# One 8 MB load per V in a decode attention kernel: longer runs, a single V buffer, and a new order of products

## The chip, the cores and the metric

The kernel runs on one core of a Trainium2 chip. The metric is device time in microseconds (us), the median of several runs. Lower is better. PE is TensorE, DVE is VectorE, ACT is ScalarE, SP is SyncE, which issues all the large loads here.

## The reference, cut to what matters

One token of a decode step is computed: attention of 32 query heads over a cache of 8 K/V heads with 32768 positions each, a small gated FFN, and a mix of both.

```python
Hq, Hkv, Sk, Dh = 32, 8, 32768, 128          # bf16; k_cache and v_cache: 64 MB each
q = (x @ wq).reshape(B, Sq, Hq, Dh)...       # wq 512 x 4096
scores = einsum("bhqd,bhkd->bhqk", q, k) * Dh ** -0.5
o = einsum("bhqk,bhkd->bhqd", softmax(scores), v)
a = o.reshape(B, Sq, Hq * Dh) @ wo           # wo 4096 x 512
b = (silu(x @ w_gate) * (x @ w_up)) @ w_down # 512 x 1792, 1792 x 512
return g * a + (1 - g) * b                   # g = sigmoid(sum(x * gate_w))
```

148 MB have to be read once, with little arithmetic on each byte.

## The kernel before

Everything large is loaded by SP in one fixed order, `stream`, into a ring of five slots of 4 MB (32 KB in each of 128 partitions). An entry whose slot was used by an earlier entry first waits until that one is released.

```python
stream = [("wq",), ("K", 0, 0), ("F1",), ("K", 0, 1), ("F2",)]
for g in range(1, G):
    for hf in range(2):
        stream += [("K", g, hf), ("V", g - 1, hf)]        # halves of K and V alternate
stream += [("V", G - 1, 0), ("V", G - 1, 1), ("wo",)]
place = {("wq",): 1, ("F1",): 4, ("wo",): 2}
for g in range(G):
    for hf in range(2):
        place["K", g, hf] = 2 * hf                        # slots 0 and 2
        place["V", g, hf] = 2 * hf + 1                    # slots 1 and 3
place["V", G - 1, 1] = 0
...
for i, e in enumerate(stream):                            # on SP, in order
    if e in before:
        sp.wait_ge(*released[before[e]])
```

`F1` is w_gate and w_up, `F2` is w_down (in memory of its own). PE takes a K half (transposes on PE, copies by DVE, scores on PE), then the products of a V half of the head before:

```python
with pe.Fori(0, G) as g:
    emit_k(0)
    with pe.If(g > 0):
        emit_pv(0)              # 32 products, V half 0 of head g - 1
    with pe.Else():
        emit_ffn()              # gate and up products
        pe.wait_ge(sem_t1, 2)
    emit_k(1)
    with pe.If(g > 0):
        emit_pv(1)
    emit_max()                  # maximum of head g: PE -> DVE -> PE -> DVE, short steps
```

After the loop come the products of the last V, the normalisation, and the products with wo, which lands in five pieces.

## Time and profile before

| | before |
|---|---|
| time, median (range) | 352.43 us (352.38 to 352.46) |
| the large DMA queue, share of 16 engines' span | 98.5% |
| PE, DVE busy | 74%, 57% |
| packets of the queue, first to last | 1.75 to 347.75 us |

The page of the profile cuts the span into 40 slices. These are, of the kernel before, the slices of PE's clock (tenths), of the DMA engines' busy share (tenths) and of the rate, and the line of the large queue (packets, MB, share of the 16 engines' span):

```profile
PEclk9999999899989698989789698989769987999899
DMA  8999999999999999999999999999999999999995
GB/s 337 441 402 434 422 440 426 443 441 422 422 437 441 430 422 426 445 441 422 422 434 445 430 422 426 441 441 422 426 422 452 434 422 426 437 445 422 413 419 207
q1 hardware_dynamic: 6050, 148.12, 98.5%
```

DMA is at 9 from the second slice to the last but one: the kernel is bound by its load queue. The chain that ended last, of the same page (shares of the span by engine, then by line), says so from the other side:

```profile
DMA 7%; PE 3%; SPq 0%; DVE 0%; issue 0%
DMA ring<-in_A_wo_dram 7%; PE ps L404 2%; PE ps L418 1%; SPq L288 0%; DVE ktT L732 0%; DVE row L824 0%; PE ps L569 0%; PE ps L465 0%
```

It is the last piece of wo, which waited its turn in the queue. Anything else on that chain is small.

The order of PE near the end, from the timeline (start us, duration us, engine, line, operation, out<-in, count):

```profile
320.38 0.63 PE L418 MATMUL ps<-ktT,qc 128*32 128x512 bf16 x8 [0.95 <-DVE ktT L732]
320.84 1.90 PE L485 MATMUL ps<-ring,ET 128*16 128x512 bf16 x32
322.67 0.27 PE L450 MATMUL ps<-ident_f,pmax 128*1 128x128 f32 x1
323.51 0.35 PE L454 MATMUL ps<-gm,ones_f 1*128 1x4 f32 x2 [0.57 <-PEq L317]
328.60 3.38 PE L485 MATMUL ps<-ring,ET 128*16 128x512 bf16 x32 [0.92 <-PEq L317]
```

The last scores of the last K half (320.38) are followed at once by the second half's 32 products of the head before (320.84). The last line is the first half of the last V: its 32 products took 3.38 us and not 1.90, after PE had hardly worked. The issues of SP in the timeline of the same kernel:

```profile
281.96 0.33 SPq L306 DMA_DIRECT2D ring<-in_A_k_cache_dram  x1
283.93 22.16 SPq L306 DMA_DIRECT2D ring<-in_A_v_cache_dram  x2
306.14 0.43 SPq L299 DMA_DIRECT2D ring<-in_A_v_cache_dram  x1
320.81 2.24 SPq L288 DMA_DIRECT2D ring<-in_A_wo_dram  x5
```

The line of 283.93 holds two issues: the second half of V(6), the V of the last head but one, at 283.93, and the first half of the last V, V(7), at 305.8 us. The second half of V(7) follows in two parts from 306.14 (one of them shown) and wo at 320.8, while the packets of V(6) are still under way until 318. The queue never runs dry.

### The profile page before, as it was taken

The page shows a single profiled execution, that of the slowest core. Times are in us where ns is not written, and L with a number is a line of the kernel's source. Part 1 is how long each engine was busy: PE and PEld are TensorE (multiplying, and loading weights), DVE is VectorE, ACT ScalarE, POOL GpSimd, SP SyncE. Part 2 cuts the span into 40 slices and gives each one's busy share as a digit, 9 for nine tenths or more (in the row PEclk, how much of TensorE's full clock was granted, in tenths as well). Part 3 has the DMA queues.
Part 4 walks back from the last instruction along what each step waited for, and adds up shares of the span by engine and source line. Part 5 has one row for each costly group of instructions (what it writes and reads, how often), then busy time and mean ns, then how long its engine had stood idle before and what let it go on. Part 6 is the DMA issues. An engine that isn't in the chain of part 4 may idle for free. (4 is left out here: it accounts for less than half of the span.)

```text
span 350.6 us, 5679 instructions
## 1 busy us (share of the span) xinstructions
PE 259.2 (74%) x2423; PEld 179.1 (51%) x2423; DVE 200.1 (57%) x368; ACT 19.9 (6%) x57; POOL 1.4 (0%) x8
## 2 busy tenths in 40 slices
PE   0449876989495886858595978858597939777686
PEld 0147153856282846546382847546474718454342
DVE  4148287779284675838283765748265926666210
ACT  1100000300100002000100001000100010000100
POOL 1000000000000000000000000000000000000000
PEclk9999999899989698989789698989769987999899
DMA  8999999999999999999999999999999999999995
GB/s 337 441 402 434 422 440 426 443 441 422 422 437 441 430 422 426 445 441 422 422 434 445 430 422 426 441 441 422 426 422 452 434 422 426 437 445 422 413 419 207
DMA packets 6060, 148.20 MB, mean 423 GB/s; under 512 B 675, under 2 KB 678, under 8 KB 1062
## 3 DMA queue, kind: packets, MB, share of 16 engines
q1 hardware_dynamic: 6050, 148.12, 98.5%
q8 instruction: 4, 0.07, 0.1%
q14 instruction: 2, 0.02, 0.0%
q10 hardware_dynamic: 4, 0.00, 0.0%
HBM read 148.11 MB, written 0.00 MB: 422 GB/s over the span
## 5 line engine op out<-in xcount | busy, mean ns | idle before, releaser
L732 DVE COPY ktT<-ps 128x1024 bf16<-128x1024 bf16 x256 | 163.1, 684 | 81.8 <-PE ps L404 79.2
L404 PE MATMUL ps<-ident_f,ring 128*128 128x128 f32 x1024 | 157.9, 310 | 48.0 <-PEq L317 48.0
L404 PEld LDWEIGHTS ps<-ident_f,ring 128*128 128x128 f32 x1024 | 132.9, 161 | 80.5 <-issue 57.1
L418 PE MATMUL ps<-ktT,qc 128*32 128x512 bf16 x512 | 41.6, 401 | 15.2 <-DVE ktT L732 15.1
L485 PE MATMUL ps<-ring,ET 128*16 128x512 bf16 x512 | 32.0, 393 | 2.8 <-PEq L317 2.1
L485 PEld LDWEIGHTS ps<-ring,ET 128*16 128x16 bf16 x512 | 12.5, 91 | 19.1 <-issue 7.6
L418 PEld LDWEIGHTS ps<-ktT,qc 128*32 128x32 bf16 x512 | 7.9, 95 | 28.0 <-DVE ktT L732 24.2
L737 DVE TENSOR_REDUCE pmaxf<-ps 128x1 f32<-128x512 f32 x16 | 11.1, 691 | 13.8 <-DVEq L736 13.8
L589 ACT ACTIVATE qc<-qz 128x112 bf16<-128x112 bf16 x8 | 2.4, 296 | 197.7 <-DVE gsel L755 194.2
L502 PEld LDWEIGHTS ps<-osel,pv_sb 128*128 128x128 f32 x80 | 11.9, 228 | 1.4 <-DVE pv_sb L773 1.0
L621 ACT ACTIVATE P<-ps,nbias 128x512 bf16<-128x512 f32 x16 | 10.8, 676 | 29.0 <-DVE gsel L755 29.0
L502 PE MATMUL ps<-osel,pv_sb 128*128 128x4 f32 x80 | 11.3, 265 | 0.8 <-DVE pv_sb L773 0.5
L773 DVE COPY pv_sb<-ps 128x512 f32<-128x512 f32 x10 | 6.8, 682 | 6.5 <-PE ps L485 6.5
L465 PE MATMUL ps<-ident,P 128*128 128x128 bf16 x72 | 7.0, 219 | 1.7 <-ACT P L621 1.2
L767 DVE COPY ET<-ps 128x512 bf16<-128x512 bf16 x18 | 7.5, 414 | 1.3 <-PE ps L465 1.3
L372 PE MATMUL ps<-ring,xT 128*1 128x448 bf16 x32 | 6.6, 984 | 0.0
L747 DVE TENSOR_REDUCE gm<-ps 1x4 f32<-1x128 f32 x8 | 2.2, 279 | 7.7 <-DVEq L746 7.7
L465 PEld LDWEIGHTS ps<-ident,P 128*128 128x128 bf16 x72 | 5.4, 98 | 2.1 <-ACT P L621 1.3
L345 PE MATMUL ps<-ring,xT 128*1 128x512 bf16 x32 | 3.6, 626 | 3.6 <-PEq L317 3.6
L454 PE MATMUL ps<-gm,ones_f 1*128 1x4 f32 x16 | 2.8, 243 | 4.6 <-PEq L317 4.6
L326 PE MATMUL ps<-ones_bf,x_row 1*128 1x1 bf16 x4 | 0.3, 173 | 7.9 <-DMA gw_row<-in_gate_w_dram 7.9
L692 DVE CAST ring<-ps 128x512 bf16<-128x512 f32 x2 | 1.3, 685 | 7.5 <-PE ps L345 7.5
(70 smaller groups left out, 50.3 us busy)
## 6 DMA issues: line engine op xcount, KB each, us to landing
ring<-in_A_k_cache_dram SPq DMA_DIRECT2D x16, 4096.0 KB, 25.1
ring<-in_A_v_cache_dram SPq DMA_DIRECT2D x15, 4096.0 KB, 32.8
ring<-in_A_wq_dram SPq DMA_DIRECT2D x1, 4096.0 KB, 12.3
ring<-in_A_v_cache_dram SPq DMA_DIRECT2D x2, 2048.0 KB, 29.4
ring<-in_A_wo_dram SPq DMA_DIRECT2D x1, 2048.0 KB, 22.4
ring<-in_B_w_gate_dram SPq DMA_DIRECT2D x1, 1792.0 KB, 25.3
ring<-in_B_w_up_dram SPq DMA_DIRECT2D x1, 1792.0 KB, 29.2
wd_t<-in_B_w_down_dram SPq DMA_DIRECT2D x1, 1792.0 KB, 43.3
```

The lines of the kernel that those rows point to most:

```text
L345: ins = pe.matmul(ps_q[i][32 * c : 32 * c + 1, :], xT[:, k : k + 1], wq_v[:, k, n0 : n0 + 512], start=(k == 0), stop=(k == KC - 1),)
L372: ins = pe.matmul(acc[32 * c : 32 * c + 1, :], xT[:, k : k + 1], wt[:, k, c * FW : (c + 1) * FW].rearrange("d (i j) -> d j i", j=FC), star ...
L404: ins = pe.transpose(stb[:, t * 64 : (t + 2) * 64], two.bitcast(FP32), ident_f[:, :])
L418: ins = pe.matmul(ps_sc[hf][32 * c : 32 * c + 32, :], qc[:, e, 24 - PB * i : 56 - PB * i], kt[:, e, :], start=(i == 0 and e == 0), stop=(i ...
L465: ins = pe.transpose(ps_pt[:, hf * 512 + m * 128 : hf * 512 + (m + 1) * 128], P[:, hf, m * 128 : (m + 1) * 128], ident[:, :],)
L485: ins = pe.matmul(ps_pv[32 * c : 32 * c + 2 * PB, :], ET[:, hf, col : col + 2 * PB], src[:, i0 : i0 + 2, c, 2 * m : 2 * m + 2, :].rearrang ...
L502: ins = pe.matmul(ps_m[:, M_OT : M_OT + HPG], pv_sb[:, r * DH : (r + 1) * DH], osel[:, r * HPG : (r + 1) * HPG], start=(r == 0), stop=(r = ...
L621: act.activation(P[:, hf, :], ps_sc[hf], ACT.Exp, bias=nbias[:, 0:1], scale=SCALE, accum_out=esum[:, g, hf : hf + 1],).then_inc(sem_exp, 1)
L732: dve.tensor_copy(ktT[:, q % NKT, :], pst[q % NST]).then_inc(sem_cp, 1)
L737: ins = dve.tensor_reduce(pmaxf[:, hf : hf + 1], ps_sc[hf], AX.X, ALU.max)
L767: dve.tensor_copy(ET[:, hf, :], ps_pt[:, hf * 512 : (hf + 1) * 512]).then_inc(sem_ptc, 1)
L773: dve.tensor_copy(pv_sb[:, :], ps_pv).then_inc(sem_pvc, 1)
```

## The change

The intent is to read V in longer runs. A V of a head becomes one load of 8 MB with 64 KB contiguous in each partition, into two neighbouring slots. For the rows of K and V to agree, a K half now holds 128 of the 256 rows of a partition (still runs of 32 KB, at a pitch of 64 KB). A V is now there only as a whole, so its products follow both K halves and the maximum. The FFN, which needs banks of PSUM (the memory that PE writes to) that the scores of head 0 use, moves behind the exponentials of head 0. wo takes the slot of wq. The last V lands in three parts.

```diff
-    stream = [("wq",), ("K", 0, 0), ("F1",), ("K", 0, 1), ("F2",)]
+    stream = [("wq",), ("K", 0, 0), ("K", 0, 1), ("F1",), ("F2",)]
     for g in range(1, G):
-        for hf in range(2):
-            stream += [("K", g, hf), ("V", g - 1, hf)]
-    stream += [("V", G - 1, 0), ("V", G - 1, 1), ("wo",)]
-    place = {("wq",): 1, ("F1",): 4, ("wo",): 2}
+        stream += [("K", g, 0), ("K", g, 1), ("V", g - 1)]
+    stream += [("V", G - 1), ("wo",)]
+    place = {("wq",): 4, ("F1",): 2, ("wo",): 4}
     for g in range(G):
-        ...                                    # K: slots 0 and 2, V: 1 and 3
+        place["K", g, 0] = 0
+        place["K", g, 1] = 1
+        place["V", g] = 2                      # and 3
+        v_slot = ring[:, 2:4, :].rearrange("p s (r d) -> p (s r) d", r=RH)
+            released[("V", g)] = (sem_pv, 2 * g + 4)      # both products
-                    elif e == ("V", 0, 1):
+                    if e == ("V", 0):
                         sp.wait_ge(sem_tT, 1)
+                        src = A_v_cache[0, e[1], :, :].rearrange("(p r) d -> p r d", r=2 * RH)
+                        if e[1] < G - 1:
+                            sp.dma_start(v_slot, src).then_inc(ld, 16)
+                            continue
+                        r0 = 0
+                        for sem, n in ((ld, RH), (sem_ldv[0], RH // 2), (sem_ldv[1], RH // 2)):
+                            ...                # the last V in three parts, into the same v_slot
                 with pe.Fori(0, G) as g:
                     emit_k(0)
+                    emit_k(1)
+                    emit_max()
                     with pe.If(g > 0):
                         emit_pv(0)
+                        emit_pv(1)
                     with pe.Else():
+                        pe.wait_ge(sem_exp, 4)
+                        pe.wait_ge(sem_ptc, 2)
                         emit_ffn()
                         pe.wait_ge(sem_t1, 2)
-                    emit_k(1)
-                    with pe.If(g > 0):
-                        emit_pv(1)
-                    emit_max()
...                                            # the FFN's steps on ACT and DVE move likewise
```

The temporaries of the FFN lie in slot 3, so V(0) also waits for the FFN's last step, the transpose that ends with `sem_tT`.

## The prediction

> **What bounds the kernel now.** The load queue. The page's queue lines show the one big queue busy 98.5% of 350.6 us (345 us of packets); the slices show DMA at 9 everywhere after the first. The DMA packets run from 1.75 to 347.75 us and never fewer than 8 of 16 engines are active for longer than 0.15 us. The chain that ended last is one wo transfer (25.6 us, queued behind V). PE (74%) and DVE (57%) are followers. So only two things can move the time: the cost of a packet, and idle time of the queue.
>
> **What the change removes.** A V load has 128 runs of 64 KB instead of 256 of 32 KB. In the trace's packets a 32 KB one takes 1218 ns, a 16 KB one 615 ns: 603 ns per 16 KB and about 13 ns fixed. Each engine carries 8 heads x 16 V packets = 128 now; 64 fewer at 13 ns give about 0.85 us (an estimate). This is all the gain there is. The Trainium skill ("DMA: Bandwidth & Descriptors", section Bandwidth) also makes the per-packet overhead matter only at small descriptors; the 13 of 1218 ns agree.
>
> **What the change adds: V has one buffer.** V(g) may be issued only when both products of V(g-1) are done. The same page (Anatomy of one DMA) says that a semaphore wait stands on the issuing sequencer before dispatch, so such a wait also stops all loads behind it.
> - Middle heads: after V lands, two K loads (19.4 us) are still to come. PE needs about 3.8 us of products, so V(g+1) is queued some 15 us early. K release is early too: K halves take PE 14.1 and 11.9 us (timeline), the cycle is 39 us. No loss.
> - Last head: V(6) and V(7) are neighbours in the queue; wo stands behind V(7) in program order. The queue must drain: landing to first product 0.47 us (337.82 to 338.29 now), two halves of products 1.9 us each (timeline, warm; one cold half took 3.4), issue to first packet 1.0 us (0.74 to 1.75), and the first packets after idling take 2.0 rather than 1.22 us. Together about 6.1 us, all on the critical path, never regained. PE should finish the maximum of head 7 just as V(6) lands, so little is added or hidden.
> - First head: V(0) waits for the FFN, which now waits for both K halves, the maximum and the exp of head 0. From the durations of now: K00 ends 37.4, K01 49.3, the bias 52.0, exp 55.2, FFN 62.0, its transpose 64.7 us; first V(0) packet about 65.9. The queue in front of it empties at 65.7. Loss about 0.9 us, uncertain: 0 to 2.5.
>
> wo in another slot, the three parts of the last V and the new K row order (same 32 KB runs, pitch 64 KB) should cost nothing. The tail after the last landing is the same.
>
> **Time:** 352.43 - 0.85 + 0.9 + 6.1 = 358.6 us, about 1.7% slower. Range 356.8 to 360.6. Faster by over 2%: 0.02; within 2%: 0.71; slower by over 2%: 0.27.
>
> **What would show it.** V packets of 64 KB near 2.42 us; a hole of about 6 us in the DMA slices around 320 us, with SyncE waiting for PE's V products just there; a hole of at most 2 us at 65 us, its wait ended by the FFN's transpose; no holes between.
>
> **What would make it wrong.** 64 KB runs that are split again (then 0.85 us is not gained); a 64 KB pitch that slows K packets (1% would cost 1.6 us); PE cold at V(6) (up to 3 us more); a later FFN; heads in the middle that lose their lead.

## More of the kernel before

The group of all V products in the page's list (count | busy us, mean ns of one | idle before):

```profile
L485 PE MATMUL ps<-ring,ET 128*16 128x512 bf16 x512 | 32.0, 393 | 2.8 <-PEq L317 2.1
```

## The result, and the profile after

| | before | after |
|---|---|---|
| time, median | 352.42 us (352.25 to 352.46, 6 runs) | 362.66 us (362.43 to 364.58, 6 runs) |
| ratio | | 1.030, 95% interval 1.028 to 1.032: slower |
| large queue, share | 98.5% | 95.5% |
| 64 matmuls of V products of head 6 | 32 behind each K half, 1.90 us | 64 in a row, 6.4 us |

A ratio here is the mean time of one kernel's fast runs over that of the other's of the same rounds, so it is not quite the ratio of the medians quoted.

The change costs 10.2 us in the medians. The predicted cost was 6.2 us, and 362.66 us lies outside the predicted range. The same lines of the page as before, of the changed kernel:

```profile
PEclk9999976579899969996899779976799889966589
DMA  8999999999999999999999999999999999908994
GB/s 343 408 459 400 434 457 412 352 462 401 390 481 397 415 426 495 397 419 426 437 444 426 419 444 437 434 419 441 412 462 405 455 408 467 455 7 347 430 417 195
q1 hardware_dynamic: 5042, 148.11, 95.5%
```

There is one slice with DMA at 0 and 7 GB/s, at 317 to 326 us, and the rate is lower in the next one. SP's own waits (issue line <- releasing engine and line: us in total, times, longest):

```profile
SPq L301 <- PE ps L486: 39.5, 1, 39.5
SPq L297 <- PE ps L486: 52.7, 6, 9.7
SPq L267 <- DVE tT L722: 15.5, 1, 15.5
```

L301 is the issue of the last V: one wait of 39.5 us, released by PE's V products, and at its end the queue had been empty for 7 us. L297 are the V loads of heads 1 to 6: the same wait, but with K loads still queued, so it costs nothing. L267 is V(0), released by the FFN's transpose. SP's issues and PE's work around the empty stretch, from the two timelines of the changed kernel:

```profile
287.07 0.33 SPq L297 DMA_DIRECT2D ring<-in_A_v_cache_dram  x1
326.93 1.28 SPq L301 DMA_DIRECT2D ring<-in_A_v_cache_dram  x3
328.25 2.55 SPq L287 DMA_DIRECT2D ring<-in_A_wo_dram  x5
```

```profile
316.59 0.64 PE L416 MATMUL ps<-ktT,qc 128*32 128x512 bf16 x8 [0.94 <-DVE ktT L735]
318.43 0.27 PE L447 MATMUL ps<-ident_f,pmax 128*1 128x128 f32 x1 [1.20 <-PEq L315]
319.28 0.55 PE L451 MATMUL ps<-gm,ones_f 1*128 1x4 f32 x2 [0.57 <-PEq L315]
320.50 6.38 PE L486 MATMUL ps<-ring,ET 128*16 128x512 bf16 x64 [0.68 <-PEq L315]
326.81 0.40 PE L462 MATMUL ps<-ident,P 128*128 128x128 bf16 x4
```

The last byte of V(6) arrived at 319.93 us. The 64 products ran from 320.50 to 326.9, the last V was issued at 326.93, and its first packet started at 327.88. The group of all V products, of the page:

```profile
L486 PE MATMUL ps<-ring,ET 128*16 128x512 bf16 x512 | 47.7, 550 | 16.9 <-PEq L315 13.7
```

The same 512 matmuls take 550 ns each in the mean, not 393 ns. Three stretches of the changed kernel, from the view by windows (stretch, length, then busy us and count of PE, PEld, DVE, ACT, POOL, then PE's granted clock, the DMA share, GB/s):

```profile
310.00:317.00 7.00, 6.05 (x63) 4.10 (x61) 6.42 (x11) 0.00 (x0) 0.00 (x0) 1.00 1.02 440
317.00:320.00 3.00, 1.05 (x8) 0.57 (x3) 1.15 (x4) 0.00 (x0) 0.00 (x0) 0.88 0.10 44
320.00:327.00 7.00, 6.50 (x68) 2.42 (x68) 0.15 (x2) 1.45 (x4) 0.00 (x0) 0.56 0.00 0
```

In the 3 us of the maximum PE works 1.05 us, and through the products that follow its clock is 0.56 in the mean. The same view, asked for finer stretches, shows the steps: from 315.87 to 319.28 us PE is busy for 0.91 of 3.41 us at a clock of 1.00, from 319.28 to 326.11 the clock is 0.50, and then 1.00 again. The clock thus fell during the maximum, 1.2 us before the first product.

Counting from the packets of the trace (start, duration and size of each), the lost time of the queue can be placed. This is a calculation, not a view of the profile: "idle" is 16 engines' time without a packet, "slow" is the time of packets beyond 13 ns + 36.8 ns per 1000 bytes (both numbers from the packets of 16 and 32 KB), each divided by 16; packets under 512 bytes are left out. Records overlap by a few nanoseconds, hence small negative numbers.

```
profiled run, us              before              after
end of the last packet        347.75              360.04
packets at full speed         345.02              344.30
60 to 70 us, idle + slow      0.04 + 0.02         1.10 + 0.74
80 to 110 us                  -0.06 - 0.01        0.38 + 0.69
310 to 330 us                 -0.05 - 0.00        8.92 + 0.67
340 us to the end             1.21 - 0.05         1.72 - 0.12
```

Three places lost time, and only the packets got cheaper. This profiled run happens to be the slowest of the six (364.58 us), so its sum is 12.3 us; the experiments below divide the 10.2 us of the medians.

The place at 60 to 70 us is V(0), from the timeline of the changed kernel:

```profile
61.38 0.54 ACT L631 ACTIVATE ring<-ps 128x448 f32<-128x448 f32 x1 [5.56 <-PE ps L370]
63.33 0.65 DVE L722 STREAM_TRANSPOSE tT<-ring 128x448 bf16<-128x448 bf16 x1
64.07 0.33 SPq L297 DMA_DIRECT2D ring<-in_A_v_cache_dram  x1
```

The FFN's gate, its transpose, and the issue of V(0) at 64.07 follow each other. The loads queued before V(0) had run out on the first engines at 63.7 us and on the last at 65.9 us.

### The profile page after: what moved, and what is told of

Read it like the earlier page. It is cut to its first block, busy times and chain, and to the rows that moved or that the text cites. A ratio compares the mean times of both kernels' runs of the same rounds, so it can differ in the third digit from the quotient of the medians.

```text
span 362.8 us, 5661 instructions
## 1 busy us (share of the span) xinstructions
PE 271.2 (75%) x2423; PEld 173.1 (48%) x2423; DVE 197.5 (54%) x368; ACT 22.6 (6%) x59; POOL 1.4 (0%) x8
## 3 DMA queue, kind: packets, MB, share of 16 engines
q1 hardware_dynamic: 5042, 148.11, 95.5%
## 5 line engine op out<-in xcount | busy, mean ns | idle before, releaser
L735 DVE COPY ktT<-ps 128x1024 bf16<-128x1024 bf16 x256 | 161.1, 683 | 77.9 <-PE ps L402 75.5
L402 PE MATMUL ps<-ident_f,ring 128*128 128x128 f32 x1024 | 149.7, 295 | 24.1 <-PEq L315 23.6
L402 PEld LDWEIGHTS ps<-ident_f,ring 128*128 128x128 f32 x1024 | 121.6, 151 | 62.2 <-issue 34.0
L486 PE MATMUL ps<-ring,ET 128*16 128x512 bf16 x512 | 47.7, 550 | 16.9 <-PEq L315 13.7
L486 PEld LDWEIGHTS ps<-ring,ET 128*16 128x16 bf16 x512 | 16.4, 118 | 43.5 <-issue 36.8
L447 PE MATMUL ps<-ident_f,pmax 128*1 128x128 f32 x8 | 2.5, 309 | 9.6 <-PEq L315 9.6
L609 ACT ACTIVATE oT<-ps 128x4 f32<-128x4 f32 x9 | 1.6, 173 | 92.6 <-PE ps L503 92.6
L451 PE MATMUL ps<-gm,ones_f 1*128 1x4 f32 x16 | 3.8, 307 | 4.6 <-PEq L315 4.6
L451 PEld LDWEIGHTS ps<-gm,ones_f 1*128 1x128 f32 x16 | 3.4, 260 | 6.4 <-issue 6.4
## 6 DMA issues: line engine op xcount, KB each, us to landing
ring<-in_A_wq_dram SPq DMA_DIRECT2D x1, 4096.0 KB, 12.3
```

The costliest lines, as they stand in the source:

```text
L402: ins = pe.transpose(stb[:, t * 64 : (t + 2) * 64], two.bitcast(FP32), ident_f[:, :])
L451: pe.matmul(ps_m[:, M_NB : M_NB + HPG], ones_f[0:1, :], gm[:, :], start=True, stop=True,).then_inc(sem_pe_nb, 1)
L486: ins = pe.matmul(ps_pv[32 * c : 32 * c + 2 * PB, :], ET[:, hf, col : col + 2 * PB], src[:, i0 : i0 + 2, c, 2 * m : 2 * m + 2, :].rearrang ...
L735: dve.tensor_copy(ktT[:, q % NKT, :], pst[q % NST]).then_inc(sem_cp, 1)
```

## The experiments

Theory A: the time goes into waits of the queue for the single V buffer (at the last head) and for the FFN (at the first), and the rest of the excess over the prediction is PE's clock in the products. Rivals: B, the 64 KB runs or the 64 KB pitch are slow by themselves; C, the V products are slow because of what they read; D, the tail of the kernel has become longer (the packets above allow 0.4 us, and from the last packet to the end of the span it is 2.8 us in both profiles). Eleven kernels were run. All gave a correct result.

### 1. The last V into other slots

```diff
-    stream += [("V", G - 1), ("wo",)]
-    place = {("wq",): 4, ("F1",): 2, ("wo",): 4}
+    stream += [("V", G - 1, 0), ("V", G - 1, 1), ("wo",)]
+    place = {("wq",): 4, ("F1",): 2, ("wo",): 1}
+    place["V", G - 1, 0] = 4        # slot of wq, long free
+    place["V", G - 1, 1] = 0        # slot of K(7, 0), free at 305 us
...                                  # SP's loads and PE's products of the last V follow
```

> The changed kernel, but the last head's V goes to other slots: its first half to the slot of wq (free since 20 us), its second half, in two parts, to the slot of K of its first half, and wo to the slot of the second K half. So no load near the end waits for the products of V of head 6. Theory A (the hole of 8 us at 320 us is a wait for the single V buffer, and nothing else): the hole closes, no stretch with all 16 engines idle after 66 us, and 8 to 9.6 us come back: 353 to 354.5 us. Rival B (64 KB runs or the 64 KB pitch are slow by themselves, or the tail is longer): at most half comes back, 357 us or more.

Measured: 353.92 us (353.69 to 354.05, and one run of 357.01), ratio 1.007 to the kernel before. SP's issues in the timeline, and the slices and the queue's line of the page:

```profile
289.83 0.33 SPq L303 DMA_DIRECT2D ring<-in_A_v_cache_dram  x1
290.21 14.34 SPq L309 DMA_DIRECT2D ring<-in_A_v_cache_dram  x3
315.70 2.23 SPq L293 DMA_DIRECT2D ring<-in_A_wo_dram  x5
```

```profile
DMA  8999999899999999999999999999999999998995
q1 hardware_dynamic: 5042, 148.11, 98.2%
```

The last V is queued from 290 us on and there is no empty slice. 8.7 us of the 10.2 come back (362.66 - 353.92). This kernel keeps the 64 KB runs, the K pitch, the order of the products and their low clock, so B and C cannot account for more than the 1.5 us that are left. Against the kernel before, measured in the same rounds, the interval of the ratio is 1.004 to 1.010.

### 2. The wait alone, in the kernel before

```diff
                     if e in before:
                         sp.wait_ge(*released[before[e]])
+                        if e == ("V", G - 1, 0):
+                            sp.wait_ge(*released[("V", G - 2, 1)])
```

> The kernel before, with one wait more: the first half of the last head's V may be issued only when both products of head 6 are done, as in the changed kernel. Nothing else differs (32 KB runs, old slots, old order). If the hole of the last head is what costs, this alone makes the old kernel slower by 5.5 to 7 us (358 to 359.5 us): V's second half lands at 318.3, its products run warm from 320.8 to 322.7, first packet about 323.7. If the cost lies in the 64 KB runs or the new order, it stays within 1 us of 352.4.

Measured: 360.82 us (360.13 to 362.40), ratio 1.024. One more wait costs the old kernel 8.3 us, more than the 5.5 to 7 expected. PE's and SP's timeline of this kernel:

```profile
321.52 0.63 PE L420 MATMUL ps<-ktT,qc 128*32 128x512 bf16 x8 [0.94 <-DVE ktT L734]
321.98 1.90 PE L487 MATMUL ps<-ring,ET 128*16 128x512 bf16 x32
```

```profile
323.99 0.33 SPq L308 DMA_DIRECT2D ring<-in_A_v_cache_dram  x1
```

The products were warm and short here, as expected (1.90 us). All engines were idle from 318.36 to 324.96 us, 6.6 us and not the 5.4 expected, since the products began at 321.98 and not at 320.8. The estimate had also left out the spread of the 16 engines: the first had finished V(6) about 2 us before the last, and from 310 to 330 us the engines lose 8.3 us idle and 0.7 us in slow packets in the mean. The wait for this load was a wait for its slowest engine, and meanwhile the others stood still, because nothing was queued behind.

So the wait alone is shown to cost about as much in the old kernel as in the changed one, but it is in part chance that 8.3 and the 8.7 us of experiment 1 are so near: here PE is busy with the scores for 3.6 us after V(6) has landed and its products are short, and in the changed kernel PE begins after 0.57 us and its products are long.

### 3. Throw-away matmuls in the waits of the maximum

```diff
                     take(sem_oc, 1)
+                    pe.wait_ge(sem_f2, 16)
+                    warm(6)                     # 512 columns each, result unused
                     take(sem_pmax, 1)
                     ...
+                    warm(3)
                     take(sem_gm, 1)
                     ...                         # second matmul of the maximum
+                    warm(3)                     # not in the later form
```

The added wait is for w_down, which the throw-away matmuls read.

> The changed kernel with twelve throw-away matmuls in the three short waits of the maximum, just before the V products. Theory: the 64 products took 6.4 us in the hole, not the 3.8 predicted, because PE had hardly worked for 3 us before them and ran at a lower clock; with PE kept busy they take 3.8 to 4.2 us (about 379 ns each in place of 631), the hole shrinks from 8 to about 5.5 us, and the time falls by 2 to 3 us, to 359.7 to 360.7. Rival: the products are slow because they read a slot of a 64 KB load or because both halves run back to back; then they stay at 6.4 us and the time stays at 362.6 or rises.

Measured: 361.97 us (360.18 to 363.53, 4 runs), ratio 1.026. The view by windows of this kernel:

```profile
317.00:321.00 4.00, 3.83 (x23) 1.32 (x23) 1.41 (x6) 0.31 (x1) 0.00 (x0) 1.00 0.08 33
321.00:325.00 4.00, 3.83 (x69) 1.83 (x68) 0.00 (x0) 1.14 (x4) 0.00 (x0) 1.00 0.00 0
```

PE's clock is 1.00 in the products, and they take 3.63 us in place of 6.38 to 6.43: the mechanism is shown, and rival C falls. The empty stretch shrank from 7.95 to 5.19 us. The time moved by 0.7 us only, and the runs scatter by 3 us, so the gain was not proved by this run. By the packets, the loss at 310 to 330 us fell only from 9.6 to 7.8 us, because in this profile the engines finished V(6) further apart (2.1 us in the mean, 1.0 in the changed kernel's). A second form, without the last three matmuls, which stood 0.7 us in the way of the products, did no better:

> The changed kernel with nine throw-away matmuls in the first two waits of the maximum and none behind it (in the first try the last three stood 0.7 us in the way of the products). Products of head 6 start at 320.4 to 320.6 and take 3.6 us again, the hole is 5.0 to 5.5 us. Expected 359.6 to 360.6 us. If it stays at 362, then what PE gains in the hole is lost in the tail of the queue, where one engine ended alone 1.8 us after the others in the profile of the changed kernel.

Measured: 362.15 us, but in two groups: 360.27, 360.40, 360.75 and 363.54, 364.32, 364.37. The profile fell into the slow group; its products took 3.63 us as expected, but began at 323.44, and the hole was 5.9 us. Its PE timeline has the first fills of head 0 (the transposes of K on PE) and the fifth group of them:

```profile
22.82 4.50 PE L402 MATMUL ps<-ident_f,ring 128*128 128x128 f32 x20 [3.94 <-PEq L315]
34.01 2.10 PE L402 MATMUL ps<-ident_f,ring 128*128 128x128 f32 x16
```

In the profile of the changed kernel these start at 22.90 and 31.12 us, and the first takes 3.75 us. In this run PE's clock came to 1.00 only at 32.0 us (25.7 in the changed kernel's), so the fifth group was 2.9 us late, the FFN came later, V(0) was issued at 66.76 us, and all 16 engines stood still from 65.77 to 67.73 us.

### 4. V in runs of 32 KB

```diff
-                            sp.dma_start(v_slot, src).then_inc(ld, 16)
+                            for r0 in (0, RH):
+                                sp.dma_start(
+                                    v_slot[:, r0 : r0 + RH, :], src[:, r0 : r0 + RH, :]
+                                ).then_inc(ld, 16)
...                                  # PE waits for both loads
```

> The changed kernel with every V load of heads 0 to 6 issued as two loads of 32 KB runs into the same two slots, both at the moment when the one load was issued. The gain of 64 KB runs by itself: 56 packets per engine and 13 ns each, 0.7 us. Expected: 363.1 to 363.5 us, 0.2% slower than the changed kernel. Rival (64 KB runs cost time): faster than the changed kernel by 1 us or more.

Measured: 363.43 us (363.01 to 366.18, 6 runs), ratio 1.033: 0.8 us slower than with 64 KB runs, though against another session's runs, and the intervals of the two ratios overlap (1.030 to 1.035 here, 1.028 to 1.032 there). The direction is that of the prediction. The rival, 1 us or more faster with 32 KB runs, falls; the other half of B, the pitch of K, is the same in both kernels and waits for experiment 6.

### 5. The FFN in head 1, in the slot of wq

```diff
-    place = {("wq",): 4, ("F1",): 2, ("wo",): 4}
+    place = {("wq",): 4, ("F1",): 4, ("wo",): 4}
-                    if e == ("V", 0):
+                    if e[0] == "wo":
                         sp.wait_ge(sem_tT, 1)
-                    with pe.Else():
+                    with pe.If(g == 1):         # behind the V products of head 0
                         ...
                         emit_ffn()
```

The FFN's temporaries move to the end of the same slot, and ACT and DVE follow in head 1.

> The changed kernel with w_gate and w_up loaded into the slot of wq and the FFN computed in head 1, behind the V products of head 0, so that V(0) waits for nothing of the FFN and PE starts head 1 at once. The hole of the last head stays. Theory A: the losses of the queue at 64 to 66 us (1.1 idle, 0.7 slow packets, mean of 16 engines) and at 90 to 100 us (0.4 and 0.6) both come from the FFN's place; without them 360 us, 2 to 3 us less than the changed kernel. If only the first was the FFN's, about 361.

Measured: 361.99 us (360.94, 361.16, 362.81, 363.77), ratio 1.029, more than either expected number. SP's timeline of this kernel:

```profile
48.52 0.43 SPq L298 DMA_DIRECT2D ring<-in_A_v_cache_dram  x1
70.02 12.28 SPq L294 DMA_DIRECT2D ring<-in_A_k_cache_dram  x2
```

V(0) is queued at 48.5 us, and by the packets the losses at 60 to 70 and at 80 to 110 us are both gone (idle and slow packets add up to less than 0.1 us). V(6) landed at 317.5 us, 2.4 us earlier than in the changed kernel's profile. So both early losses go with the FFN's place; in the second, PE, late by the FFN, released the slot of K(1, 1) late. The FFN's place makes the second loss possible, not certain: among the seven profiles with the FFN in head 0, it is 0.4 to 1.2 us in four, where PE's clock was at 0.5 for 10 to 14 us from 62 to 64 us on, and absent in two (the kernel of experiment 4 and the first of experiment 7), where the half clock lasted 3.4 us; in the seventh (the second form of experiment 3) it is 0.2 us after 10 us at half clock, there behind the stop of all engines at 66 us. In the medians only 0.7 us is gained, behind a scatter of 2.8 us; the next experiment gives more.

### 6. Both holes closed, with 64 KB and with 32 KB runs

The edits of 1 and 5 together; the second kernel has the edit of 4 as well. The wait for the FFN's transpose now stands at the last V, which takes the slot of wq.

> Both repairs together: FFN in head 1 in the slot of wq, last V in the slots of wq and of K, wo in the slot of the second K half; the V loads of heads 0 to 6 keep their 64 KB runs. If the two waits are all that the change cost, what is left is the gain of the 64 KB runs, 0.7 us: 351.5 to 352.0 us against 352.5 for the kernel before. If something of the change costs by itself (K pitch of 64 KB, order of products), it stays above 352.5.

> The kernel with both holes closed, but each V load as two loads of 32 KB runs. It should lose just the 0.7 us of the packets: 352.2 to 352.8 us, equal to the kernel before. Within 0.2 us of the kernel with 64 KB runs would say that the run length is worth nothing.

Measured: 351.84 us with 64 KB runs (four runs between 351.72 and 351.84, then 352.69 and 355.14) and 352.60 us with 32 KB runs (352.23 to 353.24), against 352.45 us for the kernel before; the ratios are 1.000 (0.997 to 1.003) and 1.000 (0.999 to 1.001). The slices and the queue's line of the first:

```profile
DMA  8999999998998999999999899999999999999994
q1 hardware_dynamic: 5042, 148.11, 98.3%
```

No slice is empty, and the queue's share is 98.3%. Its V packets of 64 KB took 2420 ns in the median, its K packets of 32 KB 1213 ns. In the medians the long runs are worth 0.76 us. The two ratios don't show it, because the outliers weigh in the means, but two other things do: of the eleven runs with both holes closed and 64 KB runs (six here, five in experiment 7) eight took 352.00 us or less, below every run of the kernel before (352.15 at the lowest); and between 115 and 300 us a packet of 64 KB took 2421 ns in the mean here, two of 32 KB in the kernel before 2 x 1217. The first head's losses are 353.92 - 351.84 = 2.1 us. With 32 KB runs and no holes the changed kernel stands 0.15 us above the kernel before, within the scatter: no cost of the K pitch or of the order of products is seen, and the rest of B falls.

### 7. A warm PE at the first K half

```diff
+                    warm_id(12)                 # 128 columns each, while q is copied
                     pe.wait_ge(sem_qs, 4)
                     ...
                     ins.then_inc(sem_pe_qe, 1)
+                    warm_id(40)                 # while the first K half lands
```

This was to test whether the scatter comes from PE's clock at the first K half, once in the changed kernel, once with the warm maximum (nine matmuls), and once with both holes closed.

> The changed kernel with throw-away matmuls of 128 columns on PE before the first K half (12 and 40 of them, in the waits from 16.8 to 22.8 us). The profiles so far show the fifth group of fills of head 0 at 31.1 us in the fast ones and at 34.0 in the slow one of the last batch: PE starts the first K half at low clock and leaves it at another moment in each run. Theory: in the changed kernel that chance goes straight into the FFN and so into the issue of V(0); with PE warm at 22.8 us that group starts at 30.5 to 31.2 us, V(0) is issued at 64.1 us or before, no run is above 363.5, the spread of the runs shrinks below 1 us (it was 2.2), median 362.0 to 362.5. Rival: the spread comes from the end of the queue or the chip; then it stays 2 us or more.

> The same, and nine throw-away matmuls in the waits of the maximum, none behind it. In the last batch this without the warm start gave two groups, 360.3 to 360.8 and 363.5 to 364.4. Theory: only the lower group is left, 359.5 to 360.8 in all runs; so warm products are worth 2.0 to 2.5 us against the kernel with the warm start alone. Rival: two groups again.

> The kernel with both holes closed, with the warm start and the throw-away matmuls of the maximum. There PE is off the critical path, so PE's clock should be worth nothing: 351.6 to 352.1 us, as without (351.84). Faster by more than 0.3 us would say that a hole is still open.

Measured, all on one chip: 363.83 us (362.24 to 365.19), 360.62 us (360.40 to 362.58) and 351.91 us (351.64 to 352.73); the kernel before had 352.37 us. The first fills of head 0 in the PE timeline of the first of them, and the V products of head 6 in the second:

```profile
22.86 2.67 PE L410 MATMUL ps<-ident_f,ring 128*128 128x128 f32 x20 [1.48 <-PEq L315]
```

```profile
319.37 3.63 PE L497 MATMUL ps<-ring,ET 128*16 128x512 bf16 x64 [0.75 <-PEq L315]
```

The fills take 2.67 us in place of 3.75 (changed kernel) or 4.50 (second form of experiment 3), and V(0) is issued at 62.8 us. Yet with the warm start alone the scatter is 3 us: that part of the theory fell. With the maximum warm too, four of five runs lie between 360.4 and 361.3 us; the fifth, 362.58, is above what was expected of all runs. On the same chip the two medians differ by 3.2 us (363.83 - 360.62), and the intervals of the ratios do not overlap (1.030 to 1.035, 1.023 to 1.027): this pair, which differs in the warm maximum alone, shows that the warm maximum saves time. How much is less sure. The products took 5.22 us in the profile of the first and 3.63 in that of the second, so about half of the difference is seen in them; the loss at 310 to 330 us is 9.3 and 6.4 us, the rest of this gap being the spread of the engines (1.9 and 0.6 us), which may be chance. Where both holes are closed, PE's clock is worth nothing, as expected: 351.91 against 351.84 us.

## Why the prediction was wrong, point by point

The direction, the three terms and their places were right; the sum was too small, because two terms were sized too small. In medians:

| term | predicted | measured | from |
|---|---|---|---|
| 64 KB runs | -0.85 | -0.76 | experiment 6 |
| first head, FFN before V(0) | +0.9 | +2.1 | 353.92 - 351.84 |
| last head, V(7) behind the products of V(6) | +6.1 | +8.7 | 362.66 - 353.92 |
| sum | +6.2 | +10.2 | 352.42 to 362.66 |

The split between the two heads depends on the order in which the medians are taken: with the first head repaired first (experiment 5) it is +0.7 (362.66 - 361.99) and +10.2 (361.99 - 351.84). The scatter of the kernels with the hole is as large as this difference. The profiles give 2.9 and 9.6 us, in the slowest of the six runs.

- **What bounds the kernel.** Right. Every change of the time, but for scatter, is idle time of the queue or the cost of its packets.
- **The last head: the step that failed most.** "Two halves of products 1.9 us each (timeline, warm; one cold half took 3.4)" took the warm duration. It measured 6.4 us for both. The prediction had read that V's products come right behind the maximum, and that the maximum ends as V(6) lands, which is what happened (319.8 and 319.9 us). It did not ask what PE does during the maximum: it works for 1.05 of 3 us, and the clock falls to half at 319.28 us, before the first product. In the kernel before, the same products follow the scores directly and are warm. This is 2.6 us of the hole in the profile (6.4 in place of 3.8). The prediction named a cold PE as a risk, but outside its sum.
- **A part that the sum did not have.** When the queue drains, the 16 engines do not finish together. In the profile of the changed kernel this adds 0.9 us idle time in the mean before the last byte of V(6) lands. The pieces of the hole then are 0.9 (spread of engines), 0.57 (landing to first product, predicted 0.47), 6.43 (products), 0.95 (issue to first packet, predicted 1.0) and 0.67 (slow first packets, predicted 0.8), 9.5 in place of 6.1 us, again in the slowest run. Experiment 2 shows the same spread in the old kernel, where it is larger.
- **The first head.** The chain was foreseen to within 1 us (the transpose ended at 64.0, predicted 64.7). The same spread of engines was missed: the first engines ran dry at 63.7, not at 65.7, and the loss there was 1.8 us in the profile. "Middle heads: no loss" failed at the second head: K(2, 1) was issued at 94.4 us, since PE was late from the FFN, and engines had run dry; 1.1 us more in this profile. From the third head on the statement holds.
- **The gain.** Right in size. The medians of experiments 4 and 6 agree on 0.8 us.
- **Not settled.** Kernels with the hole scatter by 2 to 4 us from run to run; the others mostly by about 1 us or less, with one outlier of some 3 us in two of them. A cold start of PE was seen in the profile of one slow run (the second kernel with a warm maximum), but a warm start did not end the scatter. The loss of the queue at 60 to 70 and 80 to 110 us, idle and slow together, was between 0.7 us (warm start) and 4.4 us (second form of experiment 3) in the seven profiles with the FFN in head 0, so part of the scatter lies there; but experiment 5, which has none of it, scatters by 2.8 us all the same. In the profiles of kernels with the hole one or two engines also finish 1 to 2 us behind all others, in the changed kernel from 358.2 to 360.0 us. What decides this in a run was not found.

The kernel with both holes closed is the fastest, 351.84 us, 0.6 us under the kernel before in the medians. The interval of its ratio includes 1, so this is not proved; its warmed form has 0.998 (0.997 to 1.000).

### How the Trainium skill was read

- "DMA: Bandwidth & Descriptors", section "Anatomy of one DMA", says that a semaphore wait happens on the issuing sequencer before dispatch. The traces agree: one wait on SP emptied all 16 engines, wo's loads included, for 8 us.
- "TensorE: Matmul & The Clock Gate", section "What's actually happening", says that PE's clock is halved after an idle window of about 3.4 us and restored after a busy one, and that the window runs freely, so that the moment varies from run to run. The trace agrees: the clock is 1.00 or 0.50, falls during the maximum (at 319.28 us) and stays at 1.00 there with matmuls in its waits; the first fills take 4.50, 3.75 or 2.67 us. PE was not idle before that change: it had been busy for 27% of the 3.41 us before it.

## What to carry to other kernels

A larger load saves a little per packet, but it doubles the grain of the release: check at every pair of loads that follow each other into one buffer, the last one above all, what is queued while the first is being consumed, and give the last load a slot that is already free. When a wait becomes visible in a full queue, count into it the spread of the engines, the restart of the queue, and the clock at which the consumer will really run. Moving short dependent steps (a maximum, a broadcast) in front of a matmul burst can take the clock from that burst.

## What the Trainium skill lacked or had wrong

- "DMA: Bandwidth & Descriptors", section "Bandwidth", has a cost per packet from a very small transfer issued from GpSimd (about 10.5 ns) and an overhead in cycles for packets of 256 bytes, and no time of a packet for long runs issued from SP: here 16 KB took 611 to 615 ns, 32 KB 1213 to 1218 and 64 KB 2420 ns in the median, about 13 ns a packet (two packets of 32 KB against one of 64 KB in the mean; the medians move by 5 ns between kernels), and 64 KB runs for seven V loads were worth 0.76 us of 352.
- The same page, section "Latency and other measured facts", gives about 0.6 us to the first byte of a load issued from SP. That agrees: 0.95 us from the start of the issue, of which the issue itself is 0.33. It lacks what else a queue that ran dry costs here: first packets of about 2.0 us at 32 KB and 3.1 at 64 KB in place of 1.22 and 2.42 (0.67 us in the mean of the engines), and up to 2 us of spread between the engines.
- "TensorE: Matmul & The Clock Gate" speaks of idle gaps of more than about 3 us; it gives no limit for a PE that is partly busy. Here 3.41 us with PE 27% busy in short matmuls were followed by a clock of 0.50 for 6.83 us.
- "Runtime: NRT & Kernel Launch", section "Instruction fetch mechanics", calls the cost of crossing a 16 KB block of instructions mostly hidden; in the changed kernel a 16 KB packet of an instruction queue at 348.30 us took 0.96 us, and as it ended, at 349.26 us, a packet of the load queue started that took 1.15 in place of 0.61 us. That the two shared an engine is inferred from the times, and what it does to the time of the kernel was not tested.
